# Pair 1's factors made during pair 0's first product, kept in DRAM and loaded back; the second product's totals on VectorE, its products in another order

## The chip, the cores and the metric

The kernel runs on one core of a Trainium2 chip. The time is the device time of one execution in microseconds (us). The kernel before was run three times: median 949.99 us, 949.81 to 950.48. The profile is of a further execution, of 949.58 us.

The engines by their names in the profile: PE is TensorE (PEld its weight loads), DVE is VectorE, ACT is ScalarE, POOL is GpSimd, SP is SyncE, which here only issues transfers.

## What is computed

Performer attention (random features, 4 batches, 8 heads, 576 positions) makes `x` of 2304 tokens by 512. Two feed-forward layers follow, 512 to 2048 to 512:

```python
h = x @ w_in;  g = h * np.clip(h + 3.0, 0.0, 6.0) / 6.0;       x = g @ w_out     # first layer
h = x @ w_in;  g = h * (1.0 / (1.0 + np.exp(-1.702 * h)));     out = g @ w_out   # second layer
```

The change concerns the second layer alone, which takes the last 383 us of the span.

## The kernel before

**Precision.** A matrix operand in float32 is split in two tiles of a faster type: a rounded copy `hi` (ScalarE copy) and the rest `lo = x - hi` (VectorE subtraction). Each product is three matmuls: hi*hi, hi*lo, lo*hi. Such a pair of tiles is a *factor* here.

**Strassen.** The second layer works on two batches at a time, so there are two *pairs*, p = 0 and 1. Each of its two matrix products is done by the seven products of Strassen's method (Winograd's form), numbered 1 to 7, on quarters `b11, b12, b21, b22` of the operand. In the second product 1, 7, 2 and 3 use a quarter as it is, and 6, 5 and 4 sums of quarters, made in place by `total`; in the first, 7 is such a sum too. The sums of the weights were made earlier and lie in DRAM (`sums_dram`, `left_dram`). The leftover columns of all batches (256, tile `xl`) are multiplied in the ordinary way, along with pair 1 (`rest` in the first product, `more` in the second).

**Four stages.** For each pair, `h_pair(p, u)` for u = 0 to 7 is the first product, and `o_pair(p, side)` the second.

- `x_ops(p, pool, tag)` returns steps that make the 14 factors `xop[q, op]` of a pair (two halves q of the contraction, seven operands each) from `xs`, the first layer's result in DRAM. A step is a `load` (two transfers to the raw tiles `xr`, two buffers) or a `part`: ScalarE copy L641, VectorE subtraction L642, and after four of the seven parts a `total` on GpSimd (L629 to L635). Factors lie in fixed places (`place(k)`), which pair 0 and pair 1 share. `left_x` does the same for the leftover columns (one load, four casts L590, four GpSimd subtractions L591).
- `h_pair` makes 7 products of 6 matmuls with 512 columns (L848) per u. The four weight tiles per u ("items" `a, d, c, b`) come from DRAM. The results are added up in VectorE (L881, from PSUM), and `gated` multiplies by the sigmoid (ScalarE L888; the multiplication on VectorE or GpSimd, L889, L926). The results `gt[u, e]` are the operand of the second product.
- `o_pair` makes 7 products of 8 steps; a step is 12 matmuls of 256 columns (L971), and in pair 1's products 2, 3 and 4 some more for the leftover columns. For each step `halves` splits one quarter: L946 on ScalarE, L947 on VectorE, into one of three buffers (tag `gs` of pool `gp`). In products 1, 6 and 2 each step also issues one `total` on GpSimd (L967) for the product 6, 5 or 4 that comes later. Results leave PSUM by VectorE adds L1013 and ScalarE copies and are stored. The product order is 1, 7, 6, 5, 2, 3, 4. Products 2, 3 and 4 go on summing in the PSUM banks that products 1, 5 and 7 filled.
- `split_early` makes the first three `halves` of `o_pair` ahead, inside `h_pair`.

**Order.** Weight items are loaded by SP in the fixed order of `items`, five ahead of use (`LOOK`), into six buffers (`wss`). `side()` is called after each of `o_pair`'s 56 steps; where its count is in `PLACES` it issues one step of pair 1's preparation. `behind(ins)` keeps the instructions of a step behind given instructions of the same engine. Apart from that, a pass orders each engine's queue by planned times, so work may come earlier than it is written:

```python
        turn[0] += 1
        if prep and turn[0] in PLACES:
            with behind(*split_ins):
                prep.pop(0)()
```

Of the kernel before, what the change touches and what calls it, by code (L numbers as in the profile page):

```python
# [22 lines left out]
def performer_moe_kernel(  # L23
# [13 lines left out]
    nc = tc.nc  # L37
# [105 lines left out]
    LEFT = ("11", "21", "12", "22", "s4", "s1", "s2", "s3")  # L143
    left_dram = dp.tile([P, len(LEFT), NC // 2, DM], F32, name="left")
# [458 lines left out]
    def x_ops(p, pool, tag):  # L603
# [33 lines left out]
        def part(q, k, op):  # L637
            b11, b12, b21, b22 = quarters(q)
            src = {1: b11, 2: b21, 3: b22, 7: b12, 6: b11, 5: b12, 4: b21}[op]
            s = xop[q, op] = place(k)  # L640
            nc.scalar.copy(s[:, 0], src)  # L641
            nc.vector.tensor_tensor(out=s[:, 1], in0=src, in1=s[:, 0].bitcast(F32), op=ALU.subtract)  # L642

        order = (1, 2, 3, 7, 6, 5, 4)
        steps = []
# [8 lines left out]
        return steps  # L654
# [115 lines left out]
    for p in range(B // 2):  # L770
        items += [("s", u, k_) for u in range(NC // 2) for k_ in "adcb"]
        for k_ in ("11", "s3", "s2", "s1", "12", "s4", "22"):
            more = ("11", "21") if p == B // 2 - 1 and k_ == "s4" else ()
            items += [("l", v, x) for v in range(NC // 4) for x in (k_, *more)]
    got = {}
    n_item = [0, 0]

    def fetch_to(n):
        while n_item[0] < min(n, len(items)):
            what, i, k_ = items[n_item[0]]  # L780
            if what == "s":
                s = sp.tile([P, 2, 2, DM // 2], F32R, tag="wss", bufs=6, name="wss")
                nc.sync.dma_start(out=s.bitcast(F32), in_=sums_dram[i, k_])
            else:
                s = sp.tile([P, 2, 2, DM // 2], F32R, tag="wss", bufs=6, name="wss")
                nc.sync.dma_start(
# [12 lines left out]
    for u in range(len(units) + LAG):  # L799
        while fetches and fetches[0][0] <= u + AHEAD:  # L800
            fetch_w(0, *fetches.pop(0)[1:])
        if u < len(units):
# [21 lines left out]
            if (n, c) == (B - 1, PREP):  # L824
                assert n_late[0] == len(late)
                prep = x_ops(0, wp, "w")
# [11 lines left out]
    def h_pair(p, u, first_split):  # L838
# [41 lines left out]
        def add(out, a, b):  # L880
            nc.vector.tensor_tensor(out=out, in0=a, in1=b, op=ALU.add)  # L881

        def gated(i, src, eng):
# [4 lines left out]
            nc.scalar.activation(out=g, in_=src, func=AF.Sigmoid, scale=1.702)  # L888
            eng.tensor_tensor(out=g, in0=g, in1=src, op=ALU.mult)  # L889

        last = p == B // 2 - 1
        w["a"] = next_item()
# [9 lines left out]
        gated(0, b1, nc.vector)  # L902
        if last:
# [10 lines left out]
        product(3, "d", 1, b5, False)  # L914
        c12 = temp(lp, "gs", "c12")
# [10 lines left out]
        nc.gpsimd.tensor_tensor(out=g[:, 0], in0=g[:, 1], in1=g[:, 0], op=ALU.subtract)  # L926
        if last:
# [12 lines left out]
    PLACES = (4, 10, 12, 14, 16, 26, 27, 28, 29, 30, 42, 44, 46, 48, 50, 52, 54)  # L940

    split_ins = [None, None, None]
# [9 lines left out]
    def o_pair(p, side):  # L952
# [7 lines left out]
        def total(op, u):  # L960
# [6 lines left out]
            split_ins[2] = nc.gpsimd.tensor_tensor(out=out, in0=in0, in1=in1, op=add)  # L967
# [12 lines left out]
        def product(op, ps, first):  # L980
            src = {1: 0, 7: 1, 6: 0, 5: 1, 2: 2, 3: 3, 4: 2}[op]
            ahead = {1: 6, 6: 5, 2: 4}.get(op)
            more = last and op in (2, 3, 4)
            for u in range(NC // 2):
# [3 lines left out]
                if ahead:  # L988
                    total(ahead, u)
# [39 lines left out]
        o6 = banks(psp, "ps")  # L1029
        product(6, o6, True)  # L1030
        for j in range(2):
            add(u2[j], u2[j], o6[j])
        o5 = banks(acc, "acc")
        product(5, o5, True)
        for j in range(2):
            t = temp("ob")
            add(t, u2[j], o5[j])
            add(t, t, o7[j])
            store(t, 1, j, 1)
# [3 lines left out]
        for j in range(2):  # L1043
            t = temp(("ga", "ob")[j])
            nc.scalar.copy(t, o1[j])
            store(t, 0, j, 0)
        product(3, o5, False)
# [25 lines left out]

    for p in range(B // 2):
        while prep:
            prep.pop(0)()
        for u in range(NC // 2):
            h_pair(p, u, split_early if u == NC // 2 - 1 else lambda: None)
        if p + 1 < B // 2:
            prep = x_ops(p + 1, l1, "xr") + [left_x]  # L1080

        turn = [0]

        def side():
            turn[0] += 1
            if prep and turn[0] in PLACES:
                with behind(*split_ins):
                    prep.pop(0)()

        o_pair(p, side)  # L1090
        gt.clear()
# [58 lines left out]
```

## Time and profile before

| | |
|---|---|
| median of three runs | 949.99 us (949.81 to 950.48) |
| profiled execution | 949.58 us, span 947.8 us |
| TensorE busy in the span | 920.7 us, 97% |
| VectorE busy | 609.9 us, 64% |
| ScalarE busy | 481.9 us, 51% |
| GpSimd busy | 411.5 us, 43% |
| moved by DMA | 214.07 MB, mean 226 GB/s |
| pair 0: first product, second product | 565 to 640, 640 to 738 us |
| pair 1: first product, second product | 738 to 836, 836 to 942 us |

The span is the time from the first to the last instruction on the core. Busy time counts a matmul from its start to its modelled end, and matmuls overlap, so a TensorE that is slowed a little still looks busy; a count of matmuls in a window tells more. Stage limits are read from the lines of the instructions, and stages overlap a little at their edges. The profile names for an idle engine the instruction that ended the wait.

### The profile page before, as it was taken

How to read it: one execution, taken by the hardware profiler on the slowest of the kernel's cores; microseconds unless marked ns; L12 is line 12 of the kernel's file. 1: busy time of each engine (PE TensorE's matmuls, PEld its weight loads, DVE VectorE, ACT ScalarE, POOL GpSimd, SP SyncE). 2: the span in 40 equal slices, each digit the busy share in tenths (PEclk: the TensorE clock that was granted, in tenths of full speed). 3: DMA queues.
4: the chain of work that ended last, by engine and by line, in shares of the span. 5: the costliest groups of instructions: out<-in, count | busy, mean ns of one | idle time of the engine just before them, and what ended most of it. 6: DMA issues, size and time to landing. Idle time of an engine off the chain costs nothing.

```text
span 947.8 us, 16356 instructions
## 1 busy us (share of the span) xinstructions
PE 920.7 (97%) x6238; PEld 786.5 (83%) x6238; DVE 609.9 (64%) x946; ACT 481.9 (51%) x977; POOL 411.5 (43%) x335
## 2 busy tenths in 40 slices
PE   8899999999999999999999999999899999999997
PEld 7777777778887878878888888888798888889997
DVE  7888899587585765728643344448887443387743
ACT  5887676476664765636543334334355222343442
POOL 0112222077573557636761115558554254474400
PEclk9999999999999999999999999999999999999999
DMA  6667678889888888767673447676486545565572
GB/s 204 223 230 252 240 249 273 292 297 338 300 278 291 273 300 283 265 222 262 235 280 123 145 149 254 219 222 200 133 248 197 193 163 175 161 180 175 170 255 87
DMA packets 71134, 214.07 MB, mean 226 GB/s; under 512 B 7056, under 2 KB 12816, under 8 KB 71056
## 3 DMA queue, kind: packets, MB, share of 16 engines
q1 hardware_dynamic: 70896, 212.77, 67.1%
q8 instruction: 49, 0.80, 0.4%
q10 hardware_dynamic: 160, 0.26, 0.1%
q14 instruction: 29, 0.24, 0.1%
HBM read 157.43 MB, written 55.57 MB: 225 GB/s over the span
## 4 chain that ended last, share of the span: by engine, by line
PE 76%; DVE 15%; ACT 4%; issue 2%; DMA 2%; POOL 1%; SPq 0%; POOLq 0%; DVEq 0%; ACTq 0%
PE ps L505 17%; PE h L848 16%; PE o L555 16%; PE o L971 16%; DVE gs L947 4%; PE ps L260 3%; DVE w L206 3%; PE hl L865 2%; PE ps L393 1%; POOL w L199 1%; PE ps L357 1%; DVE mx L266 1%; DVE gs L522 1%; ACT wtop L182 1%; DVE wtop L190 1%
## 5 line engine op out<-in xcount | busy, mean ns | idle before, releaser
L971 PE MATMUL o<-wss,gs 128*128 128x256 f32 x1536 | 191.7, 285 | 9.2 <-DVE gs L947 9.2
L971 PEld LDWEIGHTS o<-wss,gs 128*128 128x128 f32 x1536 | 186.6, 191 | 14.8 <-DVE gs L947 14.0
L505 PE MATMUL ps<-x,wss 128*128 128x512 f32 x768 | 193.6, 397 | 3.5 <-ACT wss L209 1.5
L505 PEld LDWEIGHTS ps<-x,wss 128*128 128x128 f32 x768 | 139.6, 188 | 35.3 <-ACT wss L209 3.1
L199 POOL TENSOR_TENSOR w<-w,wpow 128x512 f32<-128x512 f32 x64 | 78.1, 1241 | 205.6 <-DVE wpow L194 117.5
L848 PE MATMUL h<-xo,wss 128*128 128x512 f32 x672 | 160.5, 394 | 0.0
L848 PEld LDWEIGHTS h<-xo,wss 128*128 128x128 f32 x672 | 124.2, 188 | 26.1
L947 DVE TENSOR_TENSOR gs<-g,gs 128x512 fp32r<-128x512 f32 x112 | 118.7, 1085 | 38.8 <-ACT gs L946 38.8
L946 ACT CAST gs<-g 128x512 fp32r<-128x512 f32 x112 | 69.5, 621 | 96.0 <-PE o L971 88.1
L223 POOL TENSOR_TENSOR wsn<-w,wsn 128x512 fp32r<-128x512 f32 x64 | 90.3, 1427 | 50.0 <-ACT wsn L222 50.0
L555 PE MATMUL o<-gs,wsh 128*128 128x512 f32 (+1 forms) x480 | 111.7, 378 | 0.3 <-ACT gs L521 0.3
L555 PE MATMUL o<-gs,wss 128*128 128x512 f32 (+1 forms) x480 | 109.5, 374 | 2.4 <-ACT gs L521 2.4
L889 POOL TENSOR_TENSOR g<-g,c 128x512 f32<-128x512 f32 x48 | 63.9, 1332 | 104.4 <-ACT g L888 104.0
L517 DVE SCALAR_TENSOR_TENSOR ga<-ga,ps 128x512 f32<-128x512 f32 (+1 forms) x80 | 50.1, 629 | 91.7 <-ACT ga L516 91.3
L516 ACT ACTIVATE ga<-ps,three 128x512 f32<-128x512 f32 (+1 forms) x80 | 51.7, 650 | 95.1 <-PE ps L505 94.9
L967 POOL TENSOR_TENSOR g<-g 128x512 f32<-128x512 f32 x48 | 75.0, 1582 | 50.2 <-DVE gs L947 50.2
L555 PEld LDWEIGHTS o<-gs,wss 128*128 128x128 f32 x480 | 81.7, 188 | 17.4 <-ACT gs L521 3.3
L555 PEld LDWEIGHTS o<-gs,wsh 128*128 128x128 f32 x480 | 81.9, 189 | 16.1 <-ACT gs L521 1.0
L268 ACT ACTIVATE e<-ps,mx 128x128 f32<-128x128 f32 x220 | 62.7, 391 | 31.9 <-DVE mx L266 31.9
L522 DVE TENSOR_TENSOR gs<-ga,gs 128x512 fp32r<-128x512 f32 (+1 forms) x80 | 64.3, 815 | 19.7 <-ACT gs L521 18.3
L206 DVE TENSOR_TENSOR w<-w,wtop 128x512 f32<-128x512 f32 x64 | 67.0, 1057 | 11.5 <-POOL w L199 11.0
L888 ACT ACTIVATE g<-c 128x512 f32<-128x512 f32 x48 | 30.4, 632 | 82.7 <-DVE c L881 82.5
(152 smaller groups left out, 1223.1 us busy)
## 6 DMA issues: line engine op xcount, KB each, us to landing
wss<-left SPq DMA_DIRECT2D x64, 512.0 KB, 3.7
wss<-ws0i SPq DMA_DIRECT2D x48, 512.0 KB, 4.6
wraw<-in_w_in_dram SPq DMA_DIRECT2D x32, 512.0 KB, 5.0
wraw<-in_w_out_dram SPq DMA_DIRECT2D x32, 512.0 KB, 6.0
left<-wsn SPq DMA_DIRECT2D x32, 512.0 KB, 3.3
wss<-ws0o SPq DMA_DIRECT2D x24, 512.0 KB, 4.3
ws0i<-wss SPq DMA_DIRECT2D x16, 512.0 KB, 3.0
wss<-sumsa SPq DMA_DIRECT2D x16, 512.0 KB, 3.2
```

Of the source, the lines that this page charges most:

```text
L199: nc.gpsimd.tensor_tensor(out=w[:, cols], in0=w[:, cols], in1=q[:, cols], op=ALU.mult)
L206: nc.vector.tensor_tensor(out=wj, in0=wj, in1=a[:, j * DM:(j + 1) * DM], op=ALU.add)
L223: nc.gpsimd.tensor_tensor(out=s[:, :, 1], in0=t, in1=s[:, :, 0].bitcast(F32), op=ALU.subtract)
L505: nc.tensor.matmul(out=ps, lhsT=w[:, wi, kk, :], rhs=x[:, xi, kk, :], start=(m == 0), stop=(m == 3 * NK - 1),)
L522: gate[1] = nc.vector.tensor_tensor(out=s[:, 1, :], in0=g, in1=s[:, 0, :].bitcast(F32), op=ALU.subtract)
L555: nc.tensor.matmul(out=ps[:, e, :], lhsT=w[:, wi, cols], rhs=s[:, gi, :], start=(c == 0 and m == 0 and per == 1), stop=(c == NC - 1 and m ...
L848: nc.tensor.matmul(out=ps, lhsT=s[:, wi, q, :], rhs=xop[q, op][:, xi], start=(first and m == 0), stop=(m == 5), skip_group_check=not first,)
L889: eng.tensor_tensor(out=g, in0=g, in1=src, op=ALU.mult)
L946: split_ins[0] = nc.scalar.copy(s[:, 0], g)
L947: split_ins[1] = nc.vector.tensor_tensor(out=s[:, 1], in0=g, in1=s[:, 0].bitcast(F32), op=ALU.subtract)
L967: split_ins[2] = nc.gpsimd.tensor_tensor(out=out, in0=in0, in1=in1, op=add)
L971: nc.tensor.matmul(out=out, lhsT=s[:, gi, d * P:(d + 1) * P], rhs=w[:, wi, :], start=(start and m == 0), stop=(stop and m == 2), skip_grou ...
```

## The change

- Pair 1's factors are made during pair 0's `h_pair`: one step of the list at each of three calls of `side` per u, 24 turns for 17 steps. A part (`away`) goes into a `gs` buffer of `gp` and from there to a new DRAM tile `fac_dram[q, op]` (14 stores of 512 KB). `left_x` is the last step.
- During pair 0's `o_pair` a second list, `ways`, loads the 14 factors from DRAM into their places, one at every fourth step, on SP behind the latest weight item.
- `total` in `o_pair` runs on VectorE instead of GpSimd, at most one in every second step (`sums` says at which of the 56 steps), behind the latest split.
- `o_pair`'s product order becomes 1, 7, 2, 6, 5, 3, 4; weight items are reordered to match; products 6 and 5 swap PSUM pools.

```diff
+    fac_dram = {(q, op): dp.tile([P, 2, SM], F32, name=f"fac{q}{op}") for q in range(2) for op in range(1, 8)}
...
-    def x_ops(p, pool, tag):
+    def x_ops(p, pool, tag, away=False):
...
-            s = xop[q, op] = place(k)
+            if away:
+                s = gp.tile([P, 2, SM], F32R, tag="gs", bufs=3, name="xf")
+            else:
+                s = xop[q, op] = place(k)
             nc.scalar.copy(s[:, 0], src)
             nc.vector.tensor_tensor(out=s[:, 1], in0=src, in1=s[:, 0].bitcast(F32), op=ALU.subtract)
+            if away:
+                nc.sync.dma_start(out=fac_dram[q, op], in_=s.bitcast(F32))
+
+        def back(q, k, op):
+            s = xop[q, op] = place(k)
+            nc.sync.dma_start(out=s.bitcast(F32), in_=fac_dram[q, op])
...
+                ways.append(lambda q=q, k=k: back(q, 7 * q + k, order[k]))
-        return steps
+        return steps, ways
...
-        for k_ in ("11", "s3", "s2", "s1", "12", "s4", "22"):
+        for k_ in ("11", "s3", "12", "s2", "s1", "s4", "22"):
...
-    def h_pair(p, u, first_split):
+    def h_pair(p, u, side, first_split):
...
         gated(0, b1, nc.vector)
+        side(ins)
...
         product(3, "d", 1, b5, False)
+        side(ins)
...
         nc.gpsimd.tensor_tensor(out=g[:, 0], in0=g[:, 1], in1=g[:, 0], op=ALU.subtract)
+        side(ins)
...
-            split_ins[2] = nc.gpsimd.tensor_tensor(out=out, in0=in0, in1=in1, op=add)
+            nc.vector.tensor_tensor(out=out, in0=in0, in1=in1, op=add)
+
+        sums = {2 * u + 1: (6, u) for u in range(NC // 2)}
+        sums.update({2 * u + 17: (5, u) for u in range(NC // 2)})
+        sums.update({2 * u + 33: (4, u) for u in range(NC // 2)})
+        step = [0]
...
-                if ahead:
-                    total(ahead, u)
+                if step[0] in sums:
+                    with behind(*split_ins):
+                        total(*sums[step[0]])
+                step[0] += 1
...
         product(7, o7, True)
-        o6 = banks(psp, "ps")
-        product(6, o6, True)
-        for j in range(2):
-            add(u2[j], u2[j], o6[j])
-        o5 = banks(acc, "acc")
-        product(5, o5, True)
-        for j in range(2):
-            t = temp("ob")
-            add(t, u2[j], o5[j])
-            add(t, t, o7[j])
-            store(t, 1, j, 1)
...
         product(2, o1, False)
...
+        o6 = banks(acc, "acc")
+        product(6, o6, True)
+        for j in range(2):
+            add(u2[j], u2[j], o6[j])
+        o5 = banks(psp, "ps")
+        product(5, o5, True)
+        for j in range(2):
+            t = temp("ob")
+            add(t, u2[j], o5[j])
+            add(t, t, o7[j])
+            store(t, 1, j, 1)
         product(3, o5, False)
...
+    def prepare(every, *ins):
+        turn[0] += 1
+        if prep and turn[0] % every == 0:
+            with behind(*ins):
+                prep.pop(0)()
+
+    turn = [0]
     for p in range(B // 2):
         while prep:
             prep.pop(0)()
+        if p + 1 < B // 2:
+            prep, ways = x_ops(p + 1, l1, "xr", True)
+            prep.append(left_x)
         for u in range(NC // 2):
-            h_pair(p, u, split_early if u == NC // 2 - 1 else lambda: None)
-        if p + 1 < B // 2:
-            prep = x_ops(p + 1, l1, "xr") + [left_x]
...
+            end = u == NC // 2 - 1
+            h_pair(p, u, lambda ins: prepare(1, *ins), split_early if end else lambda: None)
+        prep, ways, turn[0] = ways, [], 1
+        o_pair(p, lambda: prepare(4, item_load[0]))
         gt.clear()
```

## Rows read from the trace of the kernel before

**Rows 1.** Windows by stage: length, then each engine's busy us (instructions), clock, DMA.
```profile
565.00:640.00 75.00, 75.00 (x327) 61.04 (x326) 32.62 (x49) 26.41 (x42) 40.38 (x31) 1.00 0.73 233
640.00:738.00 98.00, 90.37 (x699) 86.23 (x698) 80.45 (x81) 45.52 (x79) 56.55 (x38) 1.00 0.63 193
738.00:836.00 98.00, 98.00 (x525) 84.36 (x524) 40.98 (x60) 29.61 (x50) 41.21 (x33) 1.00 0.54 173
836.00:948.00 112.00, 104.63 (x857) 102.58 (x855) 73.56 (x88) 45.66 (x84) 37.30 (x24) 0.98 0.57 174
```

**Rows 2.** Windows, TensorE alone: length, busy us (matmuls), clock, DMA share, GB/s.
```profile
605.68:634.76 29.08, 29.08 (x128) 1.00 0.71 217
652.00:676.00 24.00, 18.06 (x133) 1.00 0.45 132
700.00:716.00 16.00, 14.32 (x115) 1.00 0.81 247
836.00:872.00 36.00, 34.39 (x270) 1.00 0.60 175
872.00:940.00 68.00, 68.00 (x573) 1.00 0.56 178
```

**Rows 3.** Groups by line, 640 to 738: busy us, mean ns, idle before and its cause.
```profile
L971 PE MATMUL o<-wss,gs 128*128 128x256 f32 x672 | 85.7, 285 | 7.6 <-DVE gs L947 7.6
...
L947 DVE TENSOR_TENSOR gs<-g,gs 128x512 fp32r<-128x512 f32 x53 | 60.0, 1163 | 12.6 <-ACT gs L946 12.6
L967 POOL TENSOR_TENSOR g<-g 128x512 f32<-128x512 f32 x21 | 34.1, 1646 | 22.5 <-DVE gs L947 22.5
...
L642 DVE TENSOR_TENSOR xo<-xr,xo 128x512 fp32r<-128x512 f32 x14 | 15.0, 1074 | 0.4 <-ACT xo L641 0.4
...
L1013 DVE TENSOR_TENSOR ob<-ob,o 128x512 f32<-128x512 f32 x10 | 6.5, 679 | 3.1 <-PE o L971 3.1
```

**Rows 4.** Groups by line, 652 to 676.
```profile
L967 POOL TENSOR_TENSOR g<-g 128x512 f32<-128x512 f32 x11 | 18.7, 1725 | 0.6 <-DVE gs L947 0.6
...
L947 DVE TENSOR_TENSOR gs<-g,gs 128x512 fp32r<-128x512 f32 x11 | 17.9, 1667 | 0.0
```

**Rows 5.** Groups by line, 908 to 940.
```profile
L947 DVE TENSOR_TENSOR gs<-g,gs 128x512 fp32r<-128x512 f32 x12 | 8.3, 693 | 13.1 <-ACT gs L946 13.0
```

**Rows 6.** Groups by line, 836 to 872.
```profile
L971 PE MATMUL o<-wss,gs 128*128 128x256 f32 x268 | 34.6, 286 | 1.6 <-DVE gs L947 1.6
```

**Rows 7.** Timeline, VectorE in pair 0's first product: start, duration, idle before and its cause.
```profile
609.78 0.69 DVE L881 TENSOR_TENSOR t<-u,h 128x512 f32<-128x512 f32 x1 [2.03 <-PE h L848]
...
613.97 0.69 DVE L881 TENSOR_TENSOR u<-p,h 128x512 f32<-128x512 f32 x1 [2.08 <-PE h L848]
...
615.37 0.69 DVE L881 TENSOR_TENSOR c<-u,h 128x512 f32<-128x512 f32 x1 [0.71 <-PE h L848]
```

**Rows 8.** Windows in pair 0's first product, as in rows 1.
```profile
565.00:570.00 5.00, 5.00 (x25) 4.08 (x24) 0.98 (x2) 1.18 (x2) 0.00 (x0) 1.00 1.02 302
575.00:580.00 5.00, 5.00 (x23) 4.02 (x23) 4.46 (x7) 3.09 (x6) 2.57 (x2) 1.00 0.97 354
605.00:635.00 30.00, 30.00 (x132) 24.44 (x131) 12.35 (x19) 9.24 (x15) 15.51 (x12) 1.00 0.69 211
```

**Rows 9.** DMA issues: count, size of one, median us from issue to landing.
```profile
left<-wsn SPq DMA_DIRECT2D x32, 512.0 KB, 3.3
...
wss<-sumsc SPq DMA_DIRECT2D x16, 512.0 KB, 4.2
...
xr<-xs SPq DMA_DIRECT2D x9, 512.0 KB, 4.8
```

**Rows 10.** Timeline, ScalarE and VectorE, three single instructions.
```profile
591.64 0.62 ACT L946 CAST gs<-g 128x512 fp32r<-128x512 f32 x1 [0.96 <-DVE g L889]
...
747.42 0.69 DVE L934 TENSOR_TENSOR gl<-gl,hl 128x512 f32<-128x512 f32 x1 [1.19 <-ACT gl L933]
...
835.73 0.39 ACT L946 CAST gs<-gl 128x256 fp32r<-128x256 f32 x1
```

More of the change, by code (lines that the diff above doesn't have):

```diff
@@ L639, in part @@
             src = {1: b11, 2: b21, 3: b22, 7: b12, 6: b11, 5: b12, 4: b21}[op]
-            s = xop[q, op] = place(k)
+            if away:
+                s = gp.tile([P, 2, SM], F32R, tag="gs", bufs=3, name="xf")
+            else:
+                s = xop[q, op] = place(k)
             nc.scalar.copy(s[:, 0], src)
             nc.vector.tensor_tensor(out=s[:, 1], in0=src, in1=s[:, 0].bitcast(F32), op=ALU.subtract)
+            if away:
[3 more added lines that the diff above has]
+            nc.sync.dma_start(out=s.bitcast(F32), in_=fac_dram[q, op])
         order = (1, 2, 3, 7, 6, 5, 4)
-        steps = []
+        steps, ways = [], []
         for q in range(2):
@@ L776, in performer_moe_kernel @@
     n_item = [0, 0]
+    item_load = [None]
     def fetch_to(n):
@@ L782, in fetch_to @@
                 s = sp.tile([P, 2, 2, DM // 2], F32R, tag="wss", bufs=6, name="wss")
-                nc.sync.dma_start(out=s.bitcast(F32), in_=sums_dram[i, k_])
+                item_load[0] = nc.sync.dma_start(out=s.bitcast(F32), in_=sums_dram[i, k_])
             else:
                 s = sp.tile([P, 2, 2, DM // 2], F32R, tag="wss", bufs=6, name="wss")
-                nc.sync.dma_start(
+                item_load[0] = nc.sync.dma_start(
                     out=s.rearrange("p u s d -> p u (s d)").bitcast(F32),
@@ L825, in performer_moe_kernel @@
                 assert n_late[0] == len(late)
-                prep = x_ops(0, wp, "w")
+                prep, _ = x_ops(0, wp, "w")
             if c == NC - 1:
@@ L880, in add @@
         def add(out, a, b):
-            nc.vector.tensor_tensor(out=out, in0=a, in1=b, op=ALU.add)
+            ins[1] = nc.vector.tensor_tensor(out=out, in0=a, in1=b, op=ALU.add)
         def gated(i, src, eng):
@@ L887, in gated @@
             g = gt[u, i // 2][:, i % 2]
-            nc.scalar.activation(out=g, in_=src, func=AF.Sigmoid, scale=1.702)
-            eng.tensor_tensor(out=g, in0=g, in1=src, op=ALU.mult)
+            ins[0] = nc.scalar.activation(out=g, in_=src, func=AF.Sigmoid, scale=1.702)
+            mul = eng.tensor_tensor(out=g, in0=g, in1=src, op=ALU.mult)
+            ins[1 if eng is nc.vector else 2] = mul
         last = p == B // 2 - 1
+        ins = [None, None, None]
         w["a"] = next_item()
@@ L939, in performer_moe_kernel @@
     ready = []
-    PLACES = (4, 10, 12, 14, 16, 26, 27, 28, 29, 30, 42, 44, 46, 48, 50, 52, 54)
-    split_ins = [None, None, None]
+    split_ins = [None, None]
     def halves(pool, N, g):
@@ L981, in product @@
             src = {1: 0, 7: 1, 6: 0, 5: 1, 2: 2, 3: 3, 4: 2}[op]
-            ahead = {1: 6, 6: 5, 2: 4}.get(op)
             more = last and op in (2, 3, 4)
@@ L1076, in performer_moe_kernel @@
             prep.pop(0)()
+        if p + 1 < B // 2:
+            prep, ways = x_ops(p + 1, l1, "xr", True)
+            prep.append(left_x)
         for u in range(NC // 2):
-            h_pair(p, u, split_early if u == NC // 2 - 1 else lambda: None)
-        if p + 1 < B // 2:
-            prep = x_ops(p + 1, l1, "xr") + [left_x]
[L1082 to L1090, printed above, removed]
+            end = u == NC // 2 - 1
+            h_pair(p, u, lambda ins: prepare(1, *ins), split_early if end else lambda: None)
+        prep, ways, turn[0] = ways, [], 1
+        o_pair(p, lambda: prepare(4, item_load[0]))
         gt.clear()
```

## The prediction

> **What bounds the kernel now.** I read the stages first, then the pace of the matmuls inside them, then what each late matmul waited for. The four windows of [rows 1] are the four stages of the last layer: pair 0's first product (565 to 640), pair 0's second product (640 to 738), and the same for pair 1 (738 to 836, 836 to 948). TensorE is busy throughout the first and third; in the second it is idle for 7.6 of 98 us, with VectorE busy 80.45 us, far above its 32.62 us in the first stage. The granted clock is 1.00 in the first three and 0.98 in the last, which holds the tail, so no clock change is at stake.
>
> A busy TensorE may still be slow, so I count matmuls. In 872 to 940, where GpSimd has little left to do, 573 matmuls of 256 columns take 68 us: 0.119 us each, 1.43 us for a step of twelve. In the first product 126 matmuls (128 with the two cut by the edges) take 29.08 us: 0.231 us each, 9.69 us for the 42 of one `u` [rows 2]. At these paces the 640 to 738 window needs 672 x 0.119 + 27 x 0.231 = 86.2 us (27 is 699 less 672 [rows 1, 3]). **Lost: 11.8 us.** Most lies in two places: 652 to 676 (133 matmuls, 15.8 us of work in 24, 8.2 lost) and 700 to 716 (13.7 in 16, 2.3 lost). In pair 1, 836 to 872 holds 268 + 2 matmuls, 32.4 us of work in 36: **3.6 us lost**; after that the pace is the undisturbed one [rows 2, 6].
>
> The idle time ahead of L971's matmuls is put down to VectorE's split subtraction, L947 [rows 3]. It takes 1667 ns in 652 to 676, where GpSimd's totals take 1725 ns [rows 4], and 693 ns where GpSimd does nothing [rows 5]. So VectorE does not have too much arithmetic: an operation with two SBUF inputs takes as long as the GpSimd operation beside it, and a 1.67 us split can't feed a 1.43 us step. The 14 subtractions L642 of pair 1's preparation stand in the same queue, 15.0 us in all [rows 3].
>
> **Part 1, second product: totals on VectorE, preparation gone.** Out of the stage go L967's GpSimd totals, L629 to L635's eight, 14 subtractions L642 (15.0 us) and 14 casts L641. VectorE gets 24 totals, two SBUF inputs like L947, so I price them at its 693 ns [rows 5]: 16.6 us. VectorE's new sum in pair 0: 56 x 0.693 + 24 x 0.693 + 10 x 0.679 (L1013) = 62.2 us in 80.0 us of matmuls [rows 3, 5]. At most every other step has a total: 3 x 0.693 = 2.08 us in two steps of 2.86 us, hidden by the matmuls. If the splits come back to 693 ns, the losses go: -11.8 and -3.6 us. At the head of both stages the last GpSimd products of the stage before still run beside the first splits; that loss lies between 0 and pair 1's whole 3.6 us per pair. I take 0.5 each, nearer to 0, since the three split buffers cover two steps: **+1.0**.
>
> **Part 2, the order 1, 7, 2, 6, 5, 3, 4.** In the old order product 3, which goes on summing in product 5's banks, comes a whole product after it; now it comes directly after. Product 5's banks must first be read by adds at 0.679 us (L1013). Bank 0 is done 6 matmuls (0.71 us) before bank 1, so its add is just covered; then come the add of product 7 and the add that frees bank 1, so three adds, 2.04 us, start 0.71 us before product 5 ends and end 1.33 us after it. Product 3's first six matmuls cover 0.71 of that; with some 0.35 us for a split that is on VectorE already, 0.95 us of wait. Bounds: nothing if the pass that orders the queues puts bank 1's add second, 2.0 if no part of the adds is covered. Taken for both pairs: **+1.9**. The reordered weight loads are as many and as large as before; item and product orders agree.
>
> **Part 3, pair 1's preparation in pair 0's first product.** There are 17 steps for 24 turns, 3.23 us apart: 14 splits, 8 totals, 4 + 1 loads, 4 + 4 small operations for the left columns, and 14 new stores of 512 KB. Engines: VectorE is busy 12.35 of 30 us, 4.0 of the 9.69 us of one `u` [rows 8]; three subtractions cost 2.1 us (at 0.693) to 5.0 us (at 1.67, as beside GpSimd [rows 4]): it fits in 5.7 us. What is queued behind such a subtraction is an add that frees a bank. The timeline shows how late that may be: `t` is added at 609.78, and the product that reuses its bank is the one whose result is added at 615.37, after the next `u`'s first two products (add at 613.97) [rows 7]; its six matmuls start 1.39 us before, near 613.9, 3.4 us after the `t` add ends. A hold-up of 1.67 us is hidden. GpSimd: 15.51 of 30 us busy, 13.4 us in the 2.67 `u` of one half of the steps; four totals at 1.73 make 20.3 of 25.8.
>
> Transfers: from turn 2 to turn 17, about 5.2 `u` or 50 us, the queue must carry 20.7 weight items, 14 stores and the second two loads: 36.7 x 0.524 = 19.2 MB. At the 354 GB/s of 575 to 580, the nearest loaded row, that is 54 us: 4 us late. At the steady row's 211 GB/s and share 0.69, so 306 GB/s if all engines were busy, it is 63 us: 13 late [rows 8]. An item is asked for when its buffer comes free, five items (12.1 us) ahead, and lands 3 to 4 us later [rows 9], so some 8 us of lateness are hidden. A store holds one of three buffers: three turns are 9.7 us, less 2.3 for copy and subtraction (0.62 and 1.67 [rows 4, 10]), against a landing of 3.3 us [rows 9] plus the lateness; there the scalar copy, and behind it the sigmoids, would wait. On SP a store that waits for its subtraction holds up the item load behind it by as much, 2.3 us, inside the 8. Turn 10 also needs the second two loads, asked for only when turn 8's subtraction has read the buffer; a load lands 4.8 us later [rows 9], two turns give 6.5. Cost between 0 and 13 - 8 = 5, more in a rival below; taken **+1.4**.
>
> The DMA page of the Trainium skill has a lower figure than its fabric ceiling for what one core gets of HBM (DMA: Bandwidth & Descriptors, Specifications: about 358 GB/s); by it the stretch would carry 19.2 MB in 54 us, and the sum would be the one above. The row of 354 GB/s at share 0.97 agrees with it.
>
> **Part 4, the 14 loads back**, one per four steps in pair 0's second product. The stage moved 193 x 98 = 18.9 MB [rows 1]; now 18.9 - 1.0 (two loads gone) + 7.3 = 25.2 MB in some 83 us: 304 GB/s, under 354. On SP each stands behind an item load and waits for nothing late: its room was last read in the first product. The last is asked for in the last step, lands some 4 us later, and is needed by the seventh product of pair 1's first `u`, six products of 6 x 0.231 or 8.3 us later. Cost 0, hidden under the five-item lead of 14 us; without that cover, the 5 us of the rival.
>
> **Sum.** The profiled execution took 949.58 us (span 947.8, 1.8 around it); the median of the runs is 949.99, 0.04% above. 949.58 - 11.8 - 3.6 + 1.0 + 1.9 + 1.4 = **938.5**.
>
> **Rivals.** (a) *Stores crowd the weight items in the first product*, but not more than half: +6 instead of +1.4, 943. For it: the 1.02 and 0.97 shares at the stage's start [rows 8]; against: the 8 us lead.
>
> (b) *Slower: the transfer engines become the bound of pair 0.* If the true rate under load is 306 GB/s, the first product is 13 us late; if scalar copies waiting for store buffers then also stop the lead from covering, all 13 reach TensorE, and the second product's 25.2 MB take 82 us with 3 us lost in bursts. 938.5 - 1.4 + 16 = 953. It decides where the 50 us stretch costs over 11 us, which is a rate below 19.2 / 61 = 315 GB/s. Against: 354 GB/s was reached.
>
> (c) *VectorE's subtraction in the first product waits for GpSimd's products and delays the adds*, so that the 14 cost 0.4 us each: 5.6 instead of 1.4, 943. For it: L642's 1074 ns mean against 693 [rows 3, 5]; against: the 3.4 us slack. The page SBUF — State Buffer (Who interferes with whom) has it as an exclusive lock, taken for a whole instruction by the one that starts first; by that rule the loss moves along with the preparation, and the 1725 and 1667 ns of [rows 4] agree that the two alternate.
>
> (d) *VectorE bounds the second product even alone*: a total ahead of a split delays it past the buffers' cover by 0.15 us, 48 times: +7, 945. Against: 2.08 of 2.86 us.
>
> (e) *The preparation isn't done in the first product at all.* It uses the split buffers, and the three early splits take these already in pair 0's first product (the third at 591.64) and hold them until 640 [rows 10]. Then most x parts fall back into the second product and share its buffers: 14 x 0.693 VectorE and slower starts, about 8 us, 946. Against: in pair 1 a split of the left columns was ready after 747.42, with its buffers free at times, yet came at 835.73, after the last other user of that ring [rows 10]: buffers are given in program order, and the x parts are first.
>
> **Chances.** Forecast 0.58; (a) 0.13; (b) 0.09; (c) 0.09; (d) 0.06; (e) 0.05. Measurements of this kernel tell about 0.2% (1.9 us) from no change. Only (b) ends slower; a (e) or (a) that is worse than priced ends near 948 to 952. Faster 0.87, same 0.04, slower 0.09. The forecast alone spans 934 (no cost in the first product, none at the bank) to 942; the range that holds 8 in 10 takes in (a), (c), (d), (e): 933.5 to 947.5.
>
> **What would show it.** Right: L947 near 0.7 us all through pair 0's second product, GpSimd empty there, windows of 24 us with about 200 matmuls, a stage of some 83 us (pair 1's 4 us shorter), the first product still near 77.5 us for its 336 matmuls, and one gap of about 1 us at the change from product 5 to 3. Wrong: gaps ahead of L848's matmuls put down to a weight load or to the bank-freeing adds (a, b, c), x parts after 640 (e), or L947 at 0.7 us with TensorE still waiting for it (d).

## The result, and the profile after

The changed kernel took 940.08 us (median of 4 runs, 939.74 to 943.56) beside 949.9 for the kernel before (4 runs, 949.56 to 950.48): a ratio of 0.9904, interval 0.988 to 0.9928. That is 9.8 us less; 938.5 us was forecast. The profiled execution is the slowest of the four, 943.56 (span 941.8), 3.5 us over the others. A second profile of the same program, the first experiment, shows where such a difference can come from.

Windows of the changed kernel by stage, answering to [rows 1]: length, busy us (instructions) of TensorE, its weight loads, VectorE, ScalarE and GpSimd, granted clock, DMA share, GB/s.

```profile
565.00:640.00 75.00, 71.79 (x305) 57.01 (x304) 45.92 (x58) 32.03 (x57) 49.64 (x37) 0.98 0.92 334
640.00:738.00 98.00, 96.74 (x747) 93.55 (x746) 65.89 (x96) 40.33 (x67) 9.84 (x7) 1.00 0.83 275
738.00:836.00 98.00, 98.00 (x531) 84.52 (x530) 42.33 (x61) 31.07 (x53) 40.38 (x32) 1.00 0.55 175
836.00:942.00 106.00, 99.75 (x832) 99.27 (x831) 64.58 (x109) 43.25 (x79) 1.33 (x1) 0.99 0.57 176
```

In pair 0's second product (640 to 738) TensorE issues 747 matmuls where it issued 699, and GpSimd's 56.55 us have shrunk to 9.84. The first product (565 to 640) paid for it: 305 matmuls where there were 327, and a DMA share of 0.92.

Groups by line of the changed kernel, 640 to 738, answering to [rows 3 to 5]. L991 is the second product's matmul line (L971 before), L962 the split (L947), L982 the total (L967, then on GpSimd), L1034 the add (L1013).

```profile
L991 PE MATMUL o<-wss,gs 128*128 128x256 f32 x672 | 82.0, 283 | 1.2 <-ACT gs L961 1.2
...
L962 DVE TENSOR_TENSOR gs<-g,gs 128x512 fp32r<-128x512 f32 x54 | 38.4, 715 | 26.0 <-ACT gs L961 24.1
...
L982 DVE TENSOR_TENSOR g<-g 128x512 f32<-128x512 f32 x24 | 18.6, 775 | 0.0
...
L1034 DVE TENSOR_TENSOR ob<-ob,o 128x512 f32<-128x512 f32 x10 | 6.5, 682 | 3.2 <-PE o L991 3.2
```

The split takes 715 ns where it took 1163, TensorE waits 1.2 us instead of 7.6, and VectorE's three sorts of work come to 63.5 us (62.2 forecast).

Timeline of TensorE in the changed kernel: start, length of an unbroken run, instructions, idle time before it and its cause. L860 is the first product's matmul line (L848 before).

```profile
565.86 16.85 PE L860 MATMUL h<-xo,wss 128*128 128x512 f32 x72
585.35 42.63 PE L860 MATMUL h<-xo,wss 128*128 128x512 f32 x174 [2.65 <-DMA wss<-sumsa]
628.54 19.99 PE L860 MATMUL h<-xo,wss 128*128 128x512 f32 x84 [0.56 <-DVE c L893]
648.36 2.20 PE L991 MATMUL o<-wss,gs 128*128 128x256 f32 x17
...
651.80 55.72 PE L991 MATMUL o<-wss,gs 128*128 128x256 f32 x463
708.76 13.67 PE L991 MATMUL o<-wss,gs 128*128 128x256 f32 x112 [1.24 <-ACT gs L961]
...
838.87 97.36 PE L991 MATMUL o<-wss,gs 128*128 128x256 f32 x812 [0.49 <-DVE gs L962]
```

Three things are to be seen. A weight item comes 2.65 us late at 585.35. At 708.76, the change from product 5 to product 3 in pair 0, there is the forecast gap, 1.24 us. And pair 1's second product has a gap of 0.49 us near its head, at 838.87, and then runs through, with none at that change.

Windows of TensorE in the changed kernel; the first is the one after the late item.

```profile
585.00:590.00 5.00, 4.65 (x13) 0.66 1.01 382
605.00:625.00 20.00, 20.00 (x87) 1.00 1.03 409
...
836.00:872.00 36.00, 35.51 (x297) 1.00 0.56 165
```

After the 2.65 us without work the granted clock is 0.66 on average, between its levels of 1.2 and 2.4 GHz, and 13 matmuls fit where 4.65 us at 0.231 each [rows 2] hold 20: 1.6 us lost beside the stall itself.

**The ledger.** As in the prediction, what a stage loses is its time less its matmuls at the undisturbed paces [rows 2]: 0.231 us for L860, 0.119 for L991 and L877. For the first product the time runs from the first L860 to the first L991; for 640 to 738 it is the window. For pair 1 it is the 36 us from where L860 gives way to L991 for good, since a fixed window would miss the head in kernels that get there earlier: 836 to 872 before, 833.07 to 869.07 in the changed kernel. The changed kernel's row: 648.36 - 565.86 - 330 x 0.231 = 6.3; 98 - 672 x 0.119 - 63 x 0.231 - 12 x 0.119 = 2.0; 36 - 296 x 0.119 = 0.8. A gap costs a little more than its idle time says, because that counts from the modelled end of the matmul before. `changed_again` is a second profiled execution of the same program; the other kernels are the experiments below. Each is one profiled execution, whose own time stands last.

| kernel | first product, pair 0 | second, pair 0 | second, pair 1 | sum | us |
|---|---|---|---|---|---|
| before | 0.1 | 11.8 | 3.6 | 15.5 | 949.58 |
| forecast | 1.4 | 1.45 | 1.45 | 4.3 | 938.5 |
| changed | 6.3 | 2.0 | 0.8 | 9.1 | 943.56 |
| changed_again | 2.9 | 2.1 | 0.8 | 5.8 | 940.04 |
| totals_gpsimd | 1.6 | 5.7 | 3.6 | 10.9 | 945.33 |
| prep_in_second | 0.1 | 4.1 | 0.8 | 5.0 | 939.64 |
| half_store | 0.6 | 2.2 | 0.8 | 3.6 | 937.62 |
| old_order | 0.8 | 0.7 | 0.9 | 2.4 | 936.53 |
| second_old | 0.1 | 2.2 | 0.9 | 3.2 | 937.39 |
| spread | 2.3 | 4.0 | 0.8 | 7.1 | 941.21 |

Time less sum is 934.0 to 934.6 in every row: the ledger accounts for the differences to about 0.6 us. The second products gave back 15.4 - 2.8 = 12.6 us in the profiled execution (12.5 forecast, the heads and the bank wait taken off); the first product took 6.3 of it, in `changed_again` 2.9.

### The profile page after: what moved, and what is told of

The parts are those of the page before. It is cut to its first block, busy times and chain, and to the rows that moved or that the text cites. A ratio compares the mean times of both kernels' runs of the same rounds, so it can differ in the third digit from the quotient of the medians.

```text
span 941.8 us, 16396 instructions
## 1 busy us (share of the span) xinstructions
PE 918.3 (98%) x6238; PEld 785.4 (83%) x6238; DVE 600.9 (64%) x994; ACT 481.2 (51%) x977; POOL 336.8 (36%) x287
## 4 chain that ended last, share of the span: by engine, by line
PE 79%; DVE 11%; ACT 4%; DMA 3%; issue 2%; POOL 1%; SPq 0%; DVEq 0%; POOLq 0%; ACTq 0%
PE o L991 19%; PE ps L506 17%; PE o L556 17%; PE h L860 14%; PE ps L261 3%; DVE w L207 3%; PE hl L877 2%; PE ps L394 1%; POOL w L200 1%; DVE mx L267 1%; PE ps L358 1%; DVE gs L523 1%; PE ps L380 1%; DVE wtop L191 1%; ACT wtop L183 1%
## 5 line engine op out<-in xcount | busy, mean ns | idle before, releaser
L991 PE MATMUL o<-wss,gs 128*128 128x256 f32 x1536 | 186.1, 283 | 1.7 <-ACT gs L961 1.2
L991 PEld LDWEIGHTS o<-wss,gs 128*128 128x128 f32 x1536 | 185.3, 190 | 2.8 <-ACT gs L961 1.4
L860 PE MATMUL h<-xo,wss 128*128 128x512 f32 x672 | 163.6, 397 | 3.2 <-DMA wss<-sumsa 2.6
L860 PEld LDWEIGHTS h<-xo,wss 128*128 128x128 f32 x672 | 124.7, 190 | 31.8 <-DMA wss<-sumsa 3.1
L962 DVE TENSOR_TENSOR gs<-g,gs 128x512 fp32r<-128x512 f32 x112 | 80.4, 721 | 57.7 <-ACT gs L961 54.6
L522 ACT CAST gs<-ga 128x512 fp32r<-128x512 f32 (+1 forms) x80 | 45.9, 581 | 12.2 <-DVE ga L518 12.1
```

The lines of the kernel that those rows point to most:

```text
L860: nc.tensor.matmul(out=ps, lhsT=s[:, wi, q, :], rhs=xop[q, op][:, xi], start=(first and m == 0), stop=(m == 5), skip_group_check=not first,)
L962: split_ins[1] = nc.vector.tensor_tensor(out=s[:, 1], in0=g, in1=s[:, 0].bitcast(F32), op=ALU.subtract)
L991: nc.tensor.matmul(out=out, lhsT=s[:, gi, d * P:(d + 1) * P], rhs=w[:, wi, :], start=(start and m == 0), stop=(stop and m == 2), skip_grou ...
```

## The experiments

Kernels 1 to 4, 5 to 8 and 9 to 12 shared a chip each; the kernel before took 949.91, 950.48 and 951.08 us on the three. Times are medians, ratios are against these. In the expectations A is the account of the prediction (splits slowed beside GpSimd, stores crowding the weight items); the other letters are rivals: B that the profiled execution's 3.5 us belong to profiling, C that what helped is the preparation's leaving the second product and not the totals' engine, D that the stores' transfers are not what costs there, E that of the new order only its gap counts, E' that this gap is a wait for a split, F that spreading the steps out changes nothing.

**1. changed_again**: the changed kernel once more, nothing edited.

> The changed kernel itself, for its spread and a second profile. The profiled execution after the change took 943.6 us, the other three 939.7 to 940.1. Theory A (transfers crowd in pair 0's first product, and one weight item that came 2.65 us late, with the low clock after it, made that execution the slow one): most executions near 940, and a profile near 940 shows no weight item waited for, and a first product of pair 0 that takes some 79 to 80 us for its 336 matmuls; one near 943.5 shows the item late again. Theory B (the 3.5 us belong to profiling): the profiled execution is near 943.5 whether or not an item is late.

940.75 (940.04 to 942.79), ratio 0.9906 [0.9891, 0.9921]. Its TensorE timeline:

```profile
583.50 25.48 PE L860 MATMUL h<-xo,wss 128*128 128x512 f32 x108 [0.86 <-DMA wss<-sumsa]
```

The same item is late by 0.86 us, not 2.65, no low clock follows, and this profiled execution is near 940: B fell. The lateness of one item varies from execution to execution. The record shows where most of the difference came from. In the changed kernel's profile ScalarE waits for one of the first layer's last stores:

```profile
573.75 0.59 ACT L910 COPY p<-h 128x512 f32<-128x512 f32 x1 [5.71 <-DMA xs<-ob]
```

In `changed_again` the same copy starts at 572.38, after 4.41 us, and what stands behind it is earlier by the same 1.4 us: the first subtraction of the preparation (577.48 and 576.11), the first factor's store, and the late item's issue behind it (578.61 and 577.23).

**2. totals_gpsimd**: the totals back on GpSimd, spaced as in the changed kernel.

```diff
-            nc.vector.tensor_tensor(out=out, in0=in0, in1=in1, op=add)
+            nc.gpsimd.tensor_tensor(out=out, in0=in0, in1=in1, op=add)
```

> The changed kernel with the second product's totals on GpSimd again; all else as changed. Theory A (splits slow down beside GpSimd's totals, so the totals' engine is what matters): splits L962 back at 1.2 to 1.4 us on average, and both second products lose about what pair 1 lost before, 3.6 us each, in place of some 1 each: 5 us more than the changed kernel, 945. Theory C (what helped is that pair 1's preparation left VectorE's queue in the second product): no more than 1 us slower than the changed kernel.

945.33 (944.51 to 946.55), ratio 0.9952 [0.9937, 0.9967]: 4.6 us slower than the changed kernel on that chip. Groups by line, 640 to 738:

```profile
L962 DVE TENSOR_TENSOR gs<-g,gs 128x512 fp32r<-128x512 f32 x54 | 59.2, 1129 | 22.5 <-ACT gs L961 22.5
L982 POOL TENSOR_TENSOR g<-g 128x512 f32<-128x512 f32 x22 | 36.6, 1695 | 0.6 <-DVE gs L962 0.6
```

The splits are back at 1129 ns and TensorE loses 5.7 and 3.6 us in the second products. A held, C fell. The engine is all that was changed. The lock that the Trainium skill describes (SBUF — State Buffer, Who interferes with whom) fits.

**3. prep_in_second**: pair 1's preparation stays in pair 0's second product, at the places of the kernel before; no store, no load back. Totals on VectorE and the new order stay.

```diff
-            prep, ways = x_ops(p + 1, l1, "xr", True)
-            prep.append(left_x)
...
-        prep, ways, turn[0] = ways, [], 1
-        o_pair(p, lambda: prepare(4, item_load[0]))
+        if p + 1 < B // 2:
+            prep = x_ops(p + 1, l1, "xr")[0] + [left_x]
+        turn[0] = 0
+        o_pair(p, lambda: in_places())
```

> Pair 1's preparation left in pair 0's second product as before (no stores, no loads back); totals on VectorE and the product order as changed. Theory A: the first product of pair 0 is back at its 77.5 us; the second one of pair 0 loses some 4 us, since eight totals of the preparation stay on GpSimd and VectorE has 62 us plus 14 subtractions of 0.7 to 1.7 us in 80; pair 1 gains its 3 us: 942, close to the changed kernel. Theory C (the preparation is what matters): pair 0's second product loses 8 us or more, 946 or more.

940.64 (939.42 to 941.92), ratio 0.9905 [0.9889, 0.9922]: the changed kernel's time, nearer to A (942) than to C (946 or more). The first product loses nothing, the second 1.73 us at one place more. Timelines there of VectorE, GpSimd and TensorE:

```profile
689.75 1.78 DVE L962 TENSOR_TENSOR gs<-g,gs 128x512 fp32r<-128x512 f32 x1
691.46 1.78 DVE L982 TENSOR_TENSOR g<-g 128x512 f32<-128x512 f32 x1
...
689.37 1.62 POOL L630 TENSOR_TENSOR xr<-xr 128x512 f32<-128x512 f32 x1 [19.75 <-DVE xo L646]
691.07 1.62 POOL L632 TENSOR_TENSOR xr<-xr 128x512 f32<-128x512 f32 x1
...
695.09 8.41 PE L991 MATMUL o<-wss,gs 128*128 128x256 f32 x68 [1.73 <-DVE gs L962]
```

The two VectorE instructions that stand beside GpSimd's two totals of x take 1.78 us. A single split beside an x total takes as long elsewhere (1.78 us at 660.67) and stops nothing; here there are two in a row. So the trip through DRAM buys back 2.0 us in the second product (4.1 and 2.1 in the ledger) and costs 2.8 in the first (0.1 and 2.9).

**4. half_store**: each factor is stored by half (7.3 MB become 3.7), and the load back fills both halves from it; the second half of each factor is left out of the computation.

```diff
-                nc.sync.dma_start(out=fac_dram[q, op], in_=s.bitcast(F32))
+                nc.sync.dma_start(out=fac_dram[q, op], in_=s[:, 0:1].bitcast(F32))
...
-            nc.sync.dma_start(out=s.bitcast(F32), in_=fac_dram[q, op])
+            nc.sync.dma_start(out=s.bitcast(F32), in_=fac_dram[q, op].to_broadcast([P, 2, SM]))
```

> Each factor's store carries only its first half (256 KB; the load back repeats that half, so the rest of each factor is left out), everything else as changed. Theory A (the first product of pair 0 pays for transfers): its loss falls by at least half, 2 us less than the changed kernel, 938. Theory D (it pays for VectorE's and GpSimd's extra work there): no change, 940.

938.28 (937.62 to 938.96), ratio 0.9877 [0.9862, 0.9891]: 2.5 us less than `changed_again`, and none of its four times reaches up to the lowest of those (940.04). The first product loses 0.6 instead of 2.9 us; that alone would say little, since `old_order`, below, keeps all stores and lost 0.8 in its profiled execution. From 575 to 625 the transfers moved 323 GB/s at share 0.91, in `changed_again` 377 at 1.00. A held.

**5. old_order**: the old product order and pools again; everything else of the change stays. Product 5's totals move with it, one on every step of product 6.

```diff
-        for k_ in ("11", "s3", "12", "s2", "s1", "s4", "22"):
+        for k_ in ("11", "s3", "s2", "s1", "12", "s4", "22"):
...
-        sums.update({2 * u + 17: (5, u) for u in range(NC // 2)})
+        sums.update({u + 16: (5, u) for u in range(NC // 2)})
...
+        o6 = banks(psp, "ps")
+        product(6, o6, True)
...
+        o5 = banks(acc, "acc")
+        product(5, o5, True)
...
         product(2, o1, False)
```

> The changed kernel with the product order of before, 1, 7, 6, 5, 2, 3, 4; the totals for product 5 then fall one on every step of product 6 (0.69 + 0.69 us of VectorE in a step of 1.43) instead of every second step of products 2 and 6. Theory A: the gap of 1.25 us at the change from product 5 to 3 goes in both pairs, and the dense totals cost about as much in and after product 6, since VectorE has 0.05 us to spare in a step and the two adds of product 6 come on top: within 2 us of the changed kernel, 938.5 to 942. Theory E (the order is free and only the gap counts): 2.5 to 3 us faster, 937.5.

938.49 (936.53 to 938.9), ratio 0.9864 [0.9847, 0.9881], beside 939.81 and 939.45 for the two kernels of the new order below, on the same chip. TensorE's timeline: the first product, then a run with products 6, 5 and 2 inside it:

```profile
565.66 77.22 PE L860 MATMUL h<-xo,wss 128*128 128x512 f32 x330
...
646.16 69.16 PE L991 MATMUL o<-wss,gs 128*128 128x256 f32 x575
```

The gap is gone, and totals on eight steps in a row cost nothing that shows. In this execution no item was late in the first product. The new order costs its one gap, 1.25 us, which is nearer to E than to A.

**6. adds_first**: both adds that free product 5's banks go ahead of product 7's adds.

```diff
-            t = temp("ob")
-            add(t, u2[j], o5[j])
-            add(t, t, o7[j])
-            store(t, 1, j, 1)
+            add(ts[j], u2[j], o5[j])
+        for j in range(2):
+            add(ts[j], ts[j], o7[j])
+            store(ts[j], 1, j, 1)
```

> The changed kernel with product 5's two bank-freeing adds ahead of the two adds of product 7's banks. Theory A (product 3 waits for those adds, bank 0 first and then bank 1): bank 1 comes free 0.68 us sooner; the wait for bank 0, which stands behind a split and a total on VectorE, stays at 1.25: 0.3 to 0.7 us per pair, 939.5. Theory E' (the gap is a wait for the split L961 that the trace names): no change, 940.4.

939.81 (938.26 to 940.63), ratio 0.9879 [0.9861, 0.9896]: a miss, since the gap that was to shrink is unchanged, 1.24 us at 704.28. Why shows in VectorE's timeline of the changed kernel, where TensorE stops at 707.52 and goes on at 708.76:

```profile
706.77 0.69 DVE L962 TENSOR_TENSOR gs<-g,gs 128x512 fp32r<-128x512 f32 x1 [0.74 <-ACT gs L961]
707.38 0.69 DVE L982 TENSOR_TENSOR g<-g 128x512 f32<-128x512 f32 x1
707.98 1.28 DVE L1034 TENSOR_TENSOR ob<-ob,o 128x512 f32<-128x512 f32 x2
709.18 0.69 DVE L962 TENSOR_TENSOR gs<-g,gs 128x512 fp32r<-128x512 f32 x1
```

By the times, TensorE goes on as the first of the two adds at 707.98 ends (0.64 each, so about 708.6): the add of bank 0, which stood behind a split and a total. The profile names ScalarE's copy (E'), but that one ends at 708.18, 0.6 us before TensorE goes on. The edit moved nothing: in `adds_first` VectorE's queue has the same two adds, a split, two adds (from 703.50, 704.69 and 705.29). Product 3 comes to bank 1 six matmuls, 0.71 us, after it goes on, and doesn't wait there, while the third add ends only at 710.4; so bank 1's add must have stood second in the changed kernel already. By its ratio this kernel is 2.4 us faster than the changed one, with the same gap and on another chip: differences of that size between chips tell nothing here.

**7. left_late**: the load of the left columns is held until behind the latest weight item.

```diff
+        with behind(item_load[0]):
-        nc.sync.dma_start(out=t, in_=xs[B].rearrange("k p s -> p k s"))
+            nc.sync.dma_start(out=t, in_=xs[B].rearrange("k p s -> p k s"))
```

> The changed kernel with the one load of the leftover columns issued behind the latest weight item at its step, in place of 574 us, where SP stood 5.9 us at it for the first layer's last store and two weight items stood behind. Theory A: the weight item that came 0.9 to 2.65 us late at 583 to 585 us comes in time, the low clock after it is gone too, and the spread of the executions with it: 1 to 3 us faster, 938.5. Theory D (extra work on VectorE and GpSimd): no change.

939.45 (938.83 to 943.76), ratio 0.9886 [0.9868, 0.9904]. The item is still late, by 0.53 us, and one of the six executions took 943.76 us: that load is not what holds it up. SyncE's timeline of the changed kernel shows what does:

```profile
574.81 0.46 SPq L795 DMA_DIRECT2D wss<-sumsc  x1
575.31 0.42 SPq L795 DMA_DIRECT2D wss<-sumsb  x1
578.19 0.32 SPq L648 DMA_DIRECT2D fac<-xf  x1
578.61 0.38 SPq L795 DMA_DIRECT2D wss<-sumsa  x1
```

The late item is issued at 578.61 behind the first store, which waits for its subtraction, and lands at 585.31; TensorE has nothing left at 582.70. In the kernel before, the same item went out at 576.41. In `changed_again` it went out at 577.23 and was late all the same, so the hold-up is not the whole of it: it took 6.2 us to land there, where items of this stage took at most 4.7 from 570 to 600 us in the kernel before. Waits of SyncE's queue in the changed kernel, 565 to 640: what waits and for what, us in total, times, longest.

```profile
SPq L648 <- DVE xf L646: 13.0, 10, 2.4
```

A store holds the item loads behind it up for as much as 2.4 us, as forecast (2.3).

**8. double_store**: each factor is stored a second time, to a tile that nobody reads (7.3 MB more).

```diff
+                nc.sync.dma_start(out=fac_more[q, op], in_=s.bitcast(F32))
```

> The changed kernel with each factor stored twice (to a second, unread tile), 7.3 MB more in pair 0's first product. Theory A: the stretch of the preparation must carry 26.5 MB, which at the 390 to 420 GB/s that the loaded windows reached is 63 to 68 us for 50; with 8 us hidden, 5 to 10 us more than the changed kernel's 3: 946 to 951. The half store gave 2.4 us back, so by a straight line through those two a full store more costs 5 us: 945. Theory D: no change, 940.5.

949.25 (948.22 to 952.09), ratio 0.9986 [0.9976, 0.9996]: 8.5 us more than `changed_again`, on another chip (7.6 by the ratios), far over the 2.5 that half a store less gave back. TensorE's timeline (L862 is L860 here):

```profile
584.95 11.42 PE L862 MATMUL h<-xo,wss 128*128 128x512 f32 x48 [0.79 <-DMA wss<-sumsa]
597.80 14.20 PE L862 MATMUL h<-xo,wss 128*128 128x512 f32 x60 [1.43 <-DMA wss<-sumsa]
617.03 18.46 PE L862 MATMUL h<-xo,wss 128*128 128x512 f32 x72 [5.04 <-DMA wss<-sumsc]
636.35 10.01 PE L862 MATMUL h<-xo,wss 128*128 128x512 f32 x42 [0.85 <-ACT p L912]
```

And the window of TensorE after the longest stall:

```profile
615.00:620.00 5.00, 2.97 (x7) 0.69 1.03 416
```

And what ScalarE's casts of the preparation (L646 here) wait for, 560 to 740: us in total, times, longest.

```profile
ACT xf L646 <- DMA fad<-xf: 6.1, 4, 2.1
```

With the DMA engines at share 1.03, item after item is late, and ScalarE's copies wait for store buffers as rival (b) had it. The first product loses 12.0 us (655.51 - 565.93 - 336 x 0.231). With one set of stores the same stretch reached share 1.00 (575 to 625, `changed_again`) and lost 2.9, so it stood close to that limit. A held, D fell.

**9. spread**: 17 steps over 22 of the 24 turns instead of the first 17.

```diff
+    def spread(ins):
+        turn[0] += 1
+        if prep and turn[0] * 17 // 22 > (turn[0] - 1) * 17 // 22:
+            with behind(*ins):
+                prep.pop(0)()
```

> The changed kernel with the 17 steps spread over 22 of the 24 turns of pair 0's first product, not the first 17. Theory A (the transfers' rate in the first half of that product is what costs): the burst from 575 us on is thinner, the stretches at 390 to 420 GB/s become fewer, and the first product's loss of about 3 us goes to 1 or less: 2 us faster than the changed kernel, ratio to before 0.989. Rival F (what costs is the transfers that pile up at the very start, the first layer's last stores and the loads, which stay): no change, 0.9905.

941.29 (941.21 to 941.51), ratio 0.9897 [0.9883, 0.9911]: it doesn't tell the two apart. TensorE's timeline:

```profile
622.70 22.64 PE L860 MATMUL h<-xo,wss 128*128 128x512 f32 x96 [1.02 <-DVE t L893]
...
652.21 53.05 PE L991 MATMUL o<-wss,gs 128*128 128x256 f32 x440 [1.67 <-DVE gs L962]
```

No matmul waits for a weight item any more, but one for an add (1.02 us), and the second product's first splits come late (1.67), as steps now run to the end of the stage.

**10. spread_old**: the edits of 9 and 5 together.

> The same spread with the product order of before. Theory A: the spread's 2 us and the 1.3 us of pair 0's gap add up: 0.987 or, if the totals on every step of product 6 cost nothing, as the trace of the old order showed, 0.9865. Rival F: as the old order alone, 0.9865 to 0.988, no better.

939.15 (938.27 to 940.24), ratio 0.9871 [0.9854, 0.9888]: 2.1 us under spread, where the gap between products 5 and 3 explains 1.25.

**11. second_old**: 3 and 5 together: only the totals' engine and spacing are left of the change.

> Nothing stored: pair 1's preparation stays in pair 0's second product, totals on VectorE, product order of before. Theory A: VectorE has 62 us of its own and 14 subtractions in 80 us, and product 6's steps now hold a split, a total and at some places a subtraction, 2.1 us in 1.43: it loses more of the second product than the 3 us with the changed order, 941 (0.990). If the order costs nothing even here, the gap goes: 939 (0.9885).

937.8 (937.39 to 939.73), ratio 0.9864 [0.9848, 0.988]: below both expectations and as fast as anything here, with no trip through DRAM. It stands 2.8 us under prep_in_second by medians, 3.9 by ratios (0.0041 of 950), on different chips, where the ledger of the profiled executions has 1.8, all of it in pair 0's second product: no gap of 1.25 us at the change of products, and 1.26 instead of 1.73 us of gap beside the x totals.

**12. half_old**: old order; one half `q` goes through DRAM, prepared at every second turn, the other is prepared in the second product.

```diff
-            if away:
+            if away and q == 0:
...
-            h_pair(p, u, lambda ins: prepare(1, *ins), split_early if end else lambda: None)
+            h_pair(p, u, lambda ins: prepare(2, *ins), split_early if end else lambda: None)
```

> Half and half: the factors of one half q made in pair 0's first product, at every second turn, and kept in DRAM (7 stores), the other half made in its second product; product order of before. Theory A: 3.7 MB stored, as many bytes as the half store, so the first product loses under 1 us; the second has 7 subtractions and 4 GpSimd totals, which slow a split each: 1 to 2 us; no gap: 937 to 938.5 (0.987), the fastest of these or level with the spread one.

937.97 (937.4 to 943.27), ratio 0.9872 [0.985, 0.9895]: no different from second_old.

## Why the prediction held, point by point

**Splits freed of GpSimd (-11.8, -3.6): right.** Split and total take 715 and 775 ns in pair 0, and all of the loss but the forecast's own small terms went. That the engine matters is shown by totals_gpsimd. But moving the totals back costs 4.6 us, not 15: in the kernel before, GpSimd had a total in each step of three products and the x totals beside them. How much of the rest is spacing and how much the x totals was not tried; prep_in_second shows only that, with the totals on VectorE, the x totals cost 1.73 us.

**Heads of the second products (+0.5 each): about right.** No gap at pair 0's; 0.49 us at pair 1's, in both executions of the changed kernel. `changed_again`:

```profile
835.46 97.24 PE L991 MATMUL o<-wss,gs 128*128 128x256 f32 x812 [0.49 <-DVE gs L962]
```

**Bank wait at product 3 (+0.95 per pair): right in place, wrong in two parts.** It is 1.25 in pair 0 and nothing in pair 1, where, by the code, product 3 begins with the matmuls of the left columns. And the add waited for is bank 0's, not bank 1's. Bank 1's stood second, the order for which the prediction had no wait at all; what it hadn't counted is a total of product 4 ahead of both.

**First product (+1.4): the term that was mis-sized**, 2.9 and 6.3. The step that failed is "some 8 us of lateness are hidden", from an item lead of 12.1 us. Already in the kernel before, the third `u`'s first item has a lead of 5.6 us: issued at 576.41, needed two products (2.8 us) ahead of the add at 584.83. The first product of the next `u` runs ahead of this one's last two, and its item is asked for only when an older one has been read. It is much the same all through that stage, as a later item of the kind shows, with ScalarE's copy that follows the item's first product (kernel before):

```profile
586.15 0.32 SPq L783 DMA_DIRECT2D wss<-sumsa  x1
...
593.16 0.59 ACT L896 COPY p<-h 128x512 f32<-128x512 f32 x1
```

The product takes six matmuls, 1.39 us, so this lead is 5.6 us too. With the landings of 3 to 4 us that the prediction had, some 2 us were hidden for these items, not 8: the lead had been counted from the number of buffers and not read. With the store ahead of it the lead of the late item shrank to 4.1 us (578.61 to 582.70), in `changed_again` to 5.4 (577.23 to 582.64), and the item took 6.7 and 6.2 to land. Later items of that kind had 8 to 12 us there, from issue to first matmul, and none stopped TensorE; one item `d` did in `changed_again`, for 0.18 us at 609.16. The landings of [rows 9] are medians of the whole execution before, with less traffic. DMA landings in the changed kernel, 572 to 640, answering to [rows 9]:

```profile
fac<-xf SPq DMA_DIRECT2D x14, 512.0 KB, 6.9
...
wss<-sumsa SPq DMA_DIRECT2D x6, 512.0 KB, 6.5
...
xr<-xs SPq DMA_DIRECT2D x3, 512.0 KB, 9.0
```

**Loads back (0): right.** In both profiles of the changed kernel no matmul of pair 0's second product waits for a weight item, at 275 GB/s.

**Rivals.** (a) is the profiled execution's story, a smaller one in the others. (b) starts to be true with doubled stores. (c) is there in traces, 0.56 us for an add at 628.54, not some 4. (d) and (e) didn't happen: VectorE kept pace, and no x part comes after 640.

**The sum.** 938.5 is 1.5 us under the profiled execution of `changed_again` (940.04), as much as the first product was mis-sized by. That the second products came out at 2.9 us, as forecast (2.1 + 0.8), is partly luck: the wait at product 3 came once and not twice, a third longer, and for another reason. The lower end of the forecast alone, 934 with no cost in the first product and none at the bank, is 935.2 by its own terms; no reading hangs on it.

What the change is worth by its parts: totals on VectorE, with their spacing, earn all of it that could be told apart (second_old, which has nothing else of the change, is 13.3 us under the kernel before); the preparation moved through DRAM changes nothing (prep_in_second), and the new order loses 1.3 us (old_order against adds_first) to 3.9 (second_old against prep_in_second, on different chips), of which the gap explains 1.25 and the rest stays open.

## What to carry to other kernels

When an engine looks too slow for its share of work, first compare its mean instruction time with the same instruction where its neighbour rests: here moving 24 sums onto the "busier" engine made it less busy (VectorE 65.9 us in pair 0's second product, 69.1 with the sums on GpSimd, in totals_gpsimd). Work moved into a stage with free engine time still has to find free transfers, and a lead counted from the number of buffers is not the lead of each item: read it from issue to first use. Undo each part of a change by itself: one of these three carried the gain, one was neutral, one cost a little.

## What the chip showed that was not expected

The transfers went to 409 GB/s over 20 us (605 to 625) and 416 over 5 us in double_store, above the 354 of [rows 8] that the forecast took for the limit. The figure of 358 that the prediction quoted from the Trainium skill is therefore no limit in this case; the Trainium skill's page HBM Reference (Specifications (TRN2)) says that a core streaming alone measures well above that share, about 425. These traces agree.

A stall of TensorE of 2.65 us was followed by a mean granted clock of 0.66 over 5 us, and one of 5.04 us stands in a window of 0.69; after one of 0.86 us, and between those of 1.68 us in the kernel before (652 to 676, [rows 2]), it stayed at 1.00. So the late transfer of 2.65 us cost TensorE its own length and then some 1.6 us more; nothing of this kind followed the shorter ones.
